# Another order for the opening steps of a fused attention and two-MLP kernel

## The chip, the cores and the metric

One core of a Trainium2 chip runs the whole program. The metric is device time in microseconds; lower is better. TensorE (PE) multiplies, VectorE (DVE), ScalarE (ACT) and GpSimd (POOL) do the rest, SyncE (SP) issues nearly all DMAs.

## The reference

```python
def _attn_ref(x, state):                      # x (4, 8, 512, 64), state (4, 8, 32, 64)
    a = softmax(scale * x @ state.T);   xread = a @ state
    a2 = softmax(scale * state @ x.T);  sread = a2 @ x
    return np.concatenate([xread, sread], axis=2)

x = attn_out.transpose(0, 2, 1, 3).reshape(2176, 512)
h = x @ w_in;   g = where(h >= 1, h, where(h <= -1, 0, (h + 1) ** 2 / 4));  x = g @ w_out   # 512 -> 2048 -> 512
h = x @ w_in2;  g = max(h, 0) + log1p(exp(-|h|));                           out = g @ w_out2
```

The four weights come as float64 and are read by the kernel as pairs of 32-bit words.

## The kernel before

**Windows.** The first MLP is done in tiles of 512 tokens (one for each of four batches and a small one), the second likewise. A tile is 16 windows of 128 hidden units. The attention of tile b is folded into the first product: for each pair p of W1 (256 hidden units) `g_mm` multiplies the state by W1 ("product p", L280), and `l1` of a window multiplies that product by the attention weights `ahi`, `alo` (L670). `l2` (L610 to L612) multiplies the activated window by W2 into four accumulators. Both products are taken in two parts, high and low: `copy` on ACT (L84) makes the high part, `sub` on DVE (L87) the low one. So product p gives `gh` and `gl`, an activated window `gth` and `gtl`, a W2 pair `wq` high and low.

**Weights.** A W1 or W2 pair (1 MB, numbered from 0) is loaded into a raw buffer, its high words are scaled by ACT (`scale`, L123), and `rebuild` on DVE shifts the low words (L138) and joins both (L139), each 128x1024. A W2 pair is then split into high and low (`split`). W1 pair p is needed by product p, W2 pair p by l2 of windows 2p and 2p+1.

**Order.** Nothing is left to a scheduler: each engine runs its instructions as they are emitted. Ahead of the loop stands block 0's attention (`f_sub` to `n_lo`) with `warm` matmuls on the identity between. Then the loop takes one step for each window i, and the lists in `ORDER` (L46) say in which order a step emits its parts: `l1` of window i, `open` (Relu and square on ACT, L759 and L760), `close` of window i-1 (the min/max on DVE, L775), `hi` and `lo` (gth, gtl of window i-1), `l2` of window i-2 (until step 14), the planned parts `early` (scale), `conv` (rebuild), `split`, `pe` (product, `place_state`) and `load`, and `hops`, pieces of the next block's attention (x transposes L305, their copies `xT`, block transposes L341 and L434, maxima and sums). `A1`, `A2` and `GW` hold the steps of the W1 pairs, the W2 pairs and the products; `HW` those of `place_state` and of the hops. The products, `place_state` (L267) and the x transposes all write the two PSUM banks of `side` (tile `at`), so each waits for the copies that empty it.

Of the kernel before, what the change touches and what calls it, by code (L numbers as in the profile page):

```python
# [10 lines left out]
F32R = mybir.dt.float32r  # L11
U32 = mybir.dt.uint32
AF = mybir.ActivationFunctionType
ALU = mybir.AluOpType
# [4 lines left out]
def fused_kernel(ctx: ExitStack, tc: tile.TileContext, x, state, w1, w2, w3, w4, out):  # L19
# [24 lines left out]
    LEAD = 14  # L44
    W_ = (7, 0, 4, 4, 4, 0, 8)
    ORDER = [  # L46
        "l1 post hops evac open close l2 early conv split hi late lo hops load pe".split(),
        "l1 post hops evac open close l2 hi split lo early conv late hops pe load".split(),
        "l1 post hops early evac open close l2 conv split hi late hops lo pe load".split(),
        "l1 post hops evac close l2 split early conv hi open late hops lo pe load".split(),  # L50
# [21 lines left out]
    def bank(tag, bufs):  # L72
        return new(psum, [P, 512], F32, tag, bufs)
# [24 lines left out]
    class Pair:  # L98
# [37 lines left out]
        def rebuild(self, v, raw):  # L136
            lo, hi, d = raw[:, 0::2], raw[:, 1::2], v.bitcast(U32)
            nc.vector.tensor_scalar(d, lo, 29, None, op0=ALU.logical_shift_right)  # L138
            nc.vector.scalar_tensor_tensor(d, hi, 3, d, op0=ALU.logical_shift_left, op1=ALU.bitwise_or)  # L139

# [23 lines left out]


    ident = new(p1, [P, P], F32, "ident")
    make_identity(nc, ident)
# [640 lines left out]

    GW = [1, 1, 2, 4, 6, 8, 10, 12]

# [3 lines left out]
    OWN = (3,)  # L814
    HW = [3, 0, 4, 15, 17]
    A1 = [-3, 0, 2, 3, 6, 6, 7, 12]
    A2 = [-1, 2, 4, 4, 8, 10, 13, 15]
    pairs, early = [], []
# [12 lines left out]
    for m, (a, pl) in enumerate(zip(at34, place)):  # L831
        w, inw, d = ((w3, True, W3), (w4, False, W4))[m % 2]
        plan_pair(Pair(w, inw, m // 2, d, lambda pl=pl: pools[pl]), a)
    pairs.sort(key=lambda t: t[0])


    room = [(-9, None), (-9, None)] + [(-9, p) for p in range(NP)]
    for n, (a, pair) in enumerate(pairs):
# [11 lines left out]
        if a == -3:  # L850
# [3 lines left out]
            continue  # L854
        when(*((a, "early") if a < NF else (a - 1, "late")), pair.scale)
        for k in range(n):
            when(a + k, "conv", lambda pair=pair, k=k, n=n: pair.conv(k, n))
        when(a + n, "split", pair.split)

# [45 lines left out]
    when(HW[0], "pe", lambda: place_state(st))  # L905
    when(0, "pe", lambda: warm(W_[5]))
    when(1, "pe", lambda: warm(W_[6]))
    for b, i0, i1 in ((1, HW[1], HW[2]), (2, NF + 3, NF + 6), (3, 2 * NF - 1, 2 * NF + 1)):
# [26 lines left out]
    with tc.manual_schedule():  # L935
# [31 lines left out]
        for g in range(NG):  # L967
            copy(hi[:, g, :], two[g][:, :C2])
        warm(W_[2], bank("acc0", 1))
        a0.scores()  # L970
        warm(W_[3], bank("acc0", 1))
        a0.f_norm(0, nc.gpsimd)
        a0.f_norm(1, nc.vector)
        run(-1, "early")
        for g in range(NG):
            a0.f_turn(g, bank(f"acc{g}", 1))
            a0.n_hi(g)
        for g in range(NG):
            sub(nc.vector, lo[:, g, :], two[g][:, :C2], f32(hi[:, g, :]))
        for g in range(NG):  # L980
            a0.s_copy(g)
        for g in range(NG):
            a0.n_lo(g, nc.vector)
        st = load_state()
        run(-1, "conv")
        run(-1, "load")

        for i in range(NW + LAG + 1):
# [6 lines left out]
            run(i, "start")  # L995
            for what in ORDER[min(i, 3) + (i >= NF)]:
                if what == "l1" and w is not None:
# [14 lines left out]
                elif what == "open" and w is not None:  # L1012
                    act_open(w)
                elif what == "hi" and v is not None:
                    cut_hi(v)
                elif what == "lo" and v is not None:
                    cut_lo(v)
                elif what in ("split", "early", "conv", "late", "pe", "load"):
                    run(i, what)
# [33 lines left out]
```

## Time and profile before

| what | us |
|---|---|
| median of 3 runs | 727.64 (727.11 to 727.82) |
| profiled execution | 727.26 |
| its span, first to last instruction | 725.5 |
| TensorE busy in the span | 715.2 (99%) |
| VectorE, ScalarE busy | 442.6 (61%), 443.6 (61%) |

Busy time of TensorE says little by itself: it counts warm-up matmuls and slow ones. What an edit of the opening can change is read from the timelines of the first 110 us: when TensorE stands, what ends the wait, and what DVE and ACT do in the meantime. In a row of a timeline, the bracket gives the idle time ahead of the group and what ended it.

### The profile page before, as it was taken

The page shows a single profiled execution, that of the slowest core. Times are in us where ns is not written, and L with a number is a line of the kernel's source. Part 1 is how long each engine was busy: PE and PEld are TensorE (multiplying, and loading weights), DVE is VectorE, ACT ScalarE, POOL GpSimd, SP SyncE. Part 2 cuts the span into 40 slices and gives each one's busy share as a digit, 9 for nine tenths or more (in the row PEclk, how much of TensorE's full clock was granted, in tenths as well). Part 3 has the DMA queues.
Part 4 walks back from the last instruction along what each step waited for, and adds up shares of the span by engine and source line. Part 5 has one row for each costly group of instructions (what it writes and reads, how often), then busy time and mean ns, then how long its engine had stood idle before and what let it go on. Part 6 is the DMA issues. An engine that isn't in the chain of part 4 may idle for free.

```text
span 725.5 us, 10280 instructions
## 1 busy us (share of the span) xinstructions
PE 715.2 (99%) x4054; PEld 579.2 (80%) x4054; DVE 442.6 (61%) x699; ACT 443.6 (61%) x730; POOL 17.9 (2%) x22
## 2 busy tenths in 40 slices
PE   8899999999999999999999999999999999999997
PEld 7577777778777887778888888888888888888886
DVE  5798875574684245777798756544555545544543
ACT  4787775555654356677887756555566556565553
POOL 0001200021000000000000000000000000000000
PEclk9999999999999999999999999999999999999999
DMA  9982005336160023353433011020002100010001
GB/s 335 349 276 104 1 0 116 61 68 108 59 175 1 1 63 112 131 174 116 148 144 130 23 37 58 11 63 0 1 1 78 39 0 1 1 58 1 1 0 59
DMA packets 61952, 56.31 MB, mean 78 GB/s; under 512 B 40976, under 2 KB 42832, under 8 KB 61904
## 3 DMA queue, kind: packets, MB, share of 16 engines
q1 hardware_dynamic: 61680, 55.46, 24.3%
q8 instruction: 32, 0.52, 0.3%
q10 hardware_dynamic: 224, 0.20, 0.1%
q14 instruction: 16, 0.13, 0.1%
HBM read 45.68 MB, written 9.96 MB: 77 GB/s over the span
## 4 chain that ended last, share of the span: by engine, by line
PE 91%; DMA 4%; DVE 2%; ACT 2%; issue 0%; SPq 0%; DVEq 0%; ACTq 0%
PE acc L610 16%; PE acc L612 16%; PE acc L611 16%; PE l L670 11%; PE l L610 9%; PE l L612 9%; PE l L611 9%; DMA wq<-in_moe_w_in_dram 3%; PE at L280 2%; PE l L657 2%; DMA ws<-in_moe_w_in_dram 1%; PE at L402 1%; ACT gh L84 0%; DVE cv L139 0%; DVE w L139 0%
## 5 line engine op out<-in xcount | busy, mean ns | idle before, releaser
L87 DVE TENSOR_TENSOR gtl<-tl,gth 128x512 fp32r<-128x512 f32 x64 | 44.3, 692 | 144.1 <-ACT gth L84 144.0
L768 ACT ACTIVATE ta<-l 128x512 f32<-128x512 f32 x68 | 40.7, 598 | 132.3 <-PE l L612 132.3
L610 PE MATMUL acc<-gth,wq 128*128 128x512 f32 x256 | 101.3, 396 | 0.0
L612 PE MATMUL acc<-gth,wq 128*128 128x512 f32 x256 | 99.8, 390 | 0.0
L611 PE MATMUL acc<-gtl,wq 128*128 128x512 f32 x256 | 99.7, 389 | 0.0
L87 DVE TENSOR_TENSOR gtl<-ta,gth 128x512 fp32r<-128x512 f32 x68 | 47.3, 695 | 66.4 <-ACT gth L84 66.4
L759 ACT ACTIVATE ta<-l 128x512 f32<-128x512 f32 x68 | 40.3, 592 | 46.7 <-PE l L670 30.2
L610 PE MATMUL acc<-wq,gth 128*128 128x512 f32 x152 | 59.2, 390 | 0.0
L611 PE MATMUL acc<-wq,gth 128*128 128x512 f32 x152 | 59.2, 389 | 0.0
L612 PE MATMUL acc<-wq,gtl 128*128 128x512 f32 x152 | 59.2, 389 | 0.0
L610 PEld LDWEIGHTS acc<-gth,wq 128*128 128x128 f32 x256 | 48.1, 188 | 12.5 <-issue 2.5
L612 PEld LDWEIGHTS acc<-gth,wq 128*128 128x128 f32 x256 | 48.0, 188 | 10.3
L611 PEld LDWEIGHTS acc<-gtl,wq 128*128 128x128 f32 x256 | 48.1, 188 | 9.5
L610 PE MATMUL acc<-wh,gth 128*128 128x512 f32 x136 | 52.9, 389 | 0.0
L611 PE MATMUL acc<-wl,gth 128*128 128x512 f32 x136 | 52.9, 389 | 0.0
L612 PE MATMUL acc<-wh,gtl 128*128 128x512 f32 x136 | 52.9, 389 | 0.0
L87 DVE TENSOR_TENSOR tl<-tl,ta 128x512 f32<-128x512 f32 x68 | 47.0, 691 | 2.4
L778 DVE SCALAR_TENSOR_TENSOR tl<-l,tl 128x512 f32<-128x512 f32 x68 | 46.4, 683 | 0.0
L779 DVE SCALAR_TENSOR_TENSOR ta<-tb,ta 128x512 f32<-128x512 f32 x68 | 46.3, 681 | 0.0
L775 DVE SCALAR_TENSOR_TENSOR ta<-ta,l 128x512 f32<-128x512 f32 x68 | 46.2, 679 | 0.0
L84 ACT ACTIVATE gth<-ta 128x512 fp32r<-128x512 f32 x68 | 42.1, 619 | 4.8 <-DVE ta L775 4.8
L771 ACT ACTIVATE tl<-tb 128x512 f32<-128x512 f32 x68 | 43.0, 633 | 2.2
(182 smaller groups left out, 1475.8 us busy)
## 6 DMA issues: line engine op xcount, KB each, us to landing
ws<-in_moe_w_in_dram SPq DMA_DIRECT2D x20, 512.0 KB, 4.6
ws<-in_moe_w_out_dram SPq DMA_DIRECT2D x20, 512.0 KB, 4.2
wq<-in_moe_w_in_dram SPq DMA_DIRECT2D x12, 512.0 KB, 8.9
wq<-in_moe_w_out_dram SPq DMA_DIRECT2D x12, 512.0 KB, 9.8
xd<-xs SPq DMA_DIRECT2D x16, 256.0 KB, 2.8
xs<-xd SPq DMA_DIRECT2D x16, 256.0 KB, 4.0
out_dram<-xs SPq DMA_DIRECT2D x15, 256.0 KB, 2.4
x<-in_x_dram SPq DMA_DIRECT2D x12, 256.0 KB, 4.5
```

The source lines that it names most:

```text
L84: nc.scalar.activation(dst, src, AF.Copy)
L87: eng.tensor_tensor(dst, a, b, op=ALU.subtract)
L610: nc.tensor.matmul(o, lh, rh, start=first, stop=False)
L611: nc.tensor.matmul(o, lh, rl, start=False, stop=False)
L612: nc.tensor.matmul(o, ll, rh, start=False, stop=last)
L670: nc.tensor.matmul(w.h, l[:, g, f], r[:, g, :], start=i == 0, stop=i == len(terms) - 1)
L759: nc.scalar.activation(w.a, w.hc, AF.Relu, bias=1.0)
L768: nc.scalar.activation(w.a, w.hc, AF.Abs)
L771: nc.scalar.activation(w.l, w.b, AF.Ln)
L775: nc.vector.scalar_tensor_tensor(w.a, w.a, 1.0, w.hc, op0=ALU.min, op1=ALU.max)
L778: nc.vector.scalar_tensor_tensor(w.l, w.hc, 0.0, w.l, op0=ALU.max, op1=ALU.add)
L779: nc.vector.scalar_tensor_tensor(w.a, w.b, 1.0, w.a, op0=ALU.subtract, op1=ALU.subtract)
```

## The change

The opening is emitted in another order, and the planned steps move. `ORDER` now has a list of its own for each of the steps 0 to 4; the lists for later steps are unchanged. In step 1 and 4 `l1` comes first, in steps 2 and 3 `l2`. `GW` puts products 1 and 2 one step later; `A1` and `A2` put W2 pair 3 from step 4 to 5, W1 pair 5 from 6 to 7 and W1 pair 6 from 7 to 9. `HW` puts `place_state` from step 3 to 5 and the hops of block 1 from 4 to 5. W1 pair 2 is loaded and rebuilt ahead of W2 pair 1. W1 pair 1's low words are shifted by ACT (`tail_act`, an ACTIVATE that reads the top byte of each low word, with a bias tile `off` that POOL sets), and the shift of W2 pair 0 stands ahead of the low parts of `alo`. The score copies `s_copy` move from ahead of the loop into step 1. The warm-up matmuls between product 0 and the scores, and those behind product 1, go; eight stand behind the scores and four at the end of step 1. Lines of the new kernel are shifted by 3 to 20 against those of the old.

```diff
@@ -10,6 +10,7 @@
 F32R = mybir.dt.float32r
 U32 = mybir.dt.uint32
+U8 = mybir.dt.uint8
 AF = mybir.ActivationFunctionType
 ALU = mybir.AluOpType
@@ -42,11 +43,13 @@
     LAG = 3
     LEAD = 14
-    W_ = (7, 0, 4, 4, 4, 0, 8)
+    W_ = (7, 8, 4)
     ORDER = [
-        "l1 post hops evac open close l2 early conv split hi late lo hops load pe".split(),
-        "l1 post hops evac open close l2 hi split lo early conv late hops pe load".split(),
-        "l1 post hops early evac open close l2 conv split hi late hops lo pe load".split(),
+        "l1 open load".split(),
+        "l1 close split hi open lo conv copy early load pe".split(),
+        "l2 close hi lo pe early l1 open conv split load".split(),
+        "l2 close hi lo pe split l1 open early conv load".split(),
+        "l1 close pe split early hi open lo l2 conv load".split(),
         "l1 post hops evac close l2 split early conv hi open late hops lo pe load".split(),
         "l1 post hops evac close l2 split early hops open hi late conv pe lo load".split(),
@@ -134,9 +137,18 @@
         def rebuild(self, v, raw):
-            lo, hi, d = raw[:, 0::2], raw[:, 1::2], v.bitcast(U32)
-            nc.vector.tensor_scalar(d, lo, 29, None, op0=ALU.logical_shift_right)
-            nc.vector.scalar_tensor_tensor(d, hi, 3, d, op0=ALU.logical_shift_left, op1=ALU.bitwise_or)
+            d = v.bitcast(U32)
+            self.tail(d, raw)
+            self.join(d, raw)
+
+        def tail(self, d, raw):
+            nc.vector.tensor_scalar(d, raw[:, 0::2], 29, None, op0=ALU.logical_shift_right)
+
+        def tail_act(self, d, raw):
+            nc.scalar.activation(d, raw.bitcast(U8)[:, 3::8], AF.Identity, scale=1.0 / 32, bias=off)
+
+        def join(self, d, raw):
+            nc.vector.scalar_tensor_tensor(d, raw[:, 1::2], 3, d, op0=ALU.logical_shift_left, op1=ALU.bitwise_or)
         def split(self):
@@ -163,6 +175,8 @@
+    off = new(p1, [P, 1], F32, "off")
+    nc.gpsimd.memset(off, 1.0 / 64 - 0.5)
     ident = new(p1, [P, P], F32, "ident")
     make_identity(nc, ident)
@@ -806,15 +820,15 @@
-    GW = [1, 1, 2, 4, 6, 8, 10, 12]
+    GW = [1, 2, 3, 4, 6, 8, 10, 12]
...
     TW.update({(3, p): 2 for p in range(0, NP, 2)})
     OWN = (3,)
-    HW = [3, 0, 4, 15, 17]
-    A1 = [-3, 0, 2, 3, 6, 6, 7, 12]
-    A2 = [-1, 2, 4, 4, 8, 10, 13, 15]
+    HW = [5, 0, 5, 15, 17]
+    A1 = [-3, 0, 2, 3, 6, 7, 9, 12]
+    A2 = [-1, 2, 4, 5, 8, 10, 13, 15]
     pairs, early = [], []
@@ -831,7 +845,8 @@
         w, inw, d = ((w3, True, W3), (w4, False, W4))[m % 2]
         plan_pair(Pair(w, inw, m // 2, d, lambda pl=pl: pools[pl]), a)
-    pairs.sort(key=lambda t: t[0])
+    pairs.sort(key=lambda t: (t[0], not t[1].inward))
+    second, third = (pairs[n][1] for n in (1, 2))
@@ -852,10 +867,13 @@
                 when(a, f"conv{i}", lambda pair=pair, i=i: pair.conv(i, 2))
             continue
-        when(*((a, "early") if a < NF else (a - 1, "late")), pair.scale)
-        for k in range(n):
-            when(a + k, "conv", lambda pair=pair, k=k, n=n: pair.conv(k, n))
-        when(a + n, "split", pair.split)
+        when(*((a - (a == 2 and pair.inward), "early") if a < NF else (a - 1, "late")), pair.scale)
+        if pair is third:
+            when(1, "conv", lambda: third.join(flat(third.v).bitcast(U32), third.raw))
+        elif pair is not second:
+            for k in range(n):
+                when(a + k, "conv", lambda pair=pair, k=k, n=n: pair.conv(k, n))
+        when(max(a + n, 1), "split", pair.split)
     def plan_g(i, b, p):
@@ -903,8 +921,8 @@
     aT0 = {}
     when(HW[0], "pe", lambda: place_state(st))
-    when(0, "pe", lambda: warm(W_[5]))
-    when(1, "pe", lambda: warm(W_[6]))
+    when(1, "pe", lambda: warm(W_[2]))
+    when(1, "copy", lambda: [a0.s_copy(g) for g in range(NG)])
     for b, i0, i1 in ((1, HW[1], HW[2]), (2, NF + 3, NF + 6), (3, 2 * NF - 1, 2 * NF + 1)):
         if b in BLOCKS:
@@ -966,23 +984,25 @@
         for g in range(NG):
             copy(hi[:, g, :], two[g][:, :C2])
-        warm(W_[2], bank("acc0", 1))
         a0.scores()
-        warm(W_[3], bank("acc0", 1))
+        warm(W_[1], bank("acc0", 1))
         a0.f_norm(0, nc.gpsimd)
         a0.f_norm(1, nc.vector)
         run(-1, "early")
+        run(0, "early")
+        third.v = W1[third.p] = new(p1, [P, NK, C2], F32, f"w1_{third.p}")
+        third.tail_act(flat(third.v).bitcast(U32), third.raw)
         for g in range(NG):
             a0.f_turn(g, bank(f"acc{g}", 1))
...
         for g in range(NG):
             sub(nc.vector, lo[:, g, :], two[g][:, :C2], f32(hi[:, g, :]))
-        for g in range(NG):
-            a0.s_copy(g)
+        second.v = new(base, [P, 1024], F32, "cv", 2)
+        second.tail(second.v.bitcast(U32), second.raw)
         for g in range(NG):
             a0.n_lo(g, nc.vector)
+        second.join(second.v.bitcast(U32), second.raw)
         st = load_state()
-        run(-1, "conv")
         run(-1, "load")
@@ -993,7 +1013,7 @@
             old = wins[i - LAG - 1] if i > LAG else None
             run(i, "start")
-            for what in ORDER[min(i, 3) + (i >= NF)]:
+            for what in ORDER[min(i, 5) + (i >= NF)]:
                 if what == "l1" and w is not None:
                     l1(w)
@@ -1015,7 +1035,7 @@
                 elif what == "lo" and v is not None:
                     cut_lo(v)
-                elif what in ("split", "early", "conv", "late", "pe", "load"):
+                elif what in ("split", "early", "conv", "late", "pe", "load", "copy"):
                     run(i, what)
             run(i, "end")
```

The first place is TensorE between the second and third window (`l`), with product 1 (`at<-w_1`), warm-up (`acc<-ident`) and l2 (`acc<-gth,wq`). Before:

```order
L670 MATMUL l_60_321<-ahi_129,gh_229 128x512 x2
L670 MATMUL l_60_321<-ahi_129,gl_230 128x512 x2
L670 MATMUL l_60_321<-alo_130,gh_229 128x512 x2
L280 MATMUL at_69<-w_1_56_309,stT_4_76 32x256 x8
L212 MATMUL acc_66_348<-ident_70 128x128 x8
L670 MATMUL l_67_357<-ahi_129,gh_344 128x512 x2
L670 MATMUL l_67_357<-ahi_129,gl_345 128x512 x2
L670 MATMUL l_67_357<-alo_130,gh_344 128x512 x2
L610 MATMUL acc_69_370<-gth_332,wq_57_312 128x512
```

And now, from the last matmuls of the first l2 on (its twelve, and four warm-ups ahead of them, follow the second window directly):

```order
L624 MATMUL acc_67_354<-gth_324,wq_57_321 128x512
L625 MATMUL acc_67_354<-gtl_325,wq_57_321 128x512
L626 MATMUL acc_67_354<-gth_324,wq_57_321 128x512
L294 MATMUL at_69<-w_1_48_272,stT_5_78 32x256 x8
L684 MATMUL l_72_376<-ahi_131,gh_371 128x512 x2
L684 MATMUL l_72_376<-ahi_131,gl_372 128x512 x2
L684 MATMUL l_72_376<-alo_132,gh_371 128x512 x2
L624 MATMUL acc_64_342<-gth_359,wq_57_321 128x512
```

The first l2 has moved ahead of product 1 and the third window, which it followed.

The second place is TensorE in steps 3 to 5: product 3 (`at<-w_3`) and `place_state` (`at<-ident,xs`). Before, in steps 3 to 4, `place_state` stood between l2 and window 4:

```order
L612 MATMUL acc_72_382<-gth_392,wq_57_312 128x512
L267 MATMUL at_69<-ident_70,xs_290 128x128 x4
L670 MATMUL l_87_453<-ahi_129,gh_404 128x512 x2
L670 MATMUL l_87_453<-ahi_129,gl_405 128x512 x2
L670 MATMUL l_87_453<-alo_130,gh_404 128x512 x2
L305 MATMUL at_69<-ident_70,x_58_315 128x128 x8
L610 MATMUL acc_69_370<-gth_438,wq_81_431 128x512
```

Now two windows follow product 2, and product 3 stands behind them, ahead of the l2 of window 2:

```order
L294 MATMUL at_69<-w_2_74_386,stT_5_78 32x256 x8
L684 MATMUL l_82_427<-ahi_131,gh_371 128x512 x2
L684 MATMUL l_82_427<-ahi_131,gl_372 128x512 x2
L684 MATMUL l_82_427<-alo_132,gh_371 128x512 x2
L684 MATMUL l_86_444<-ahi_131,gh_420 128x512 x2
L684 MATMUL l_86_444<-ahi_131,gl_421 128x512 x2
L684 MATMUL l_86_444<-alo_132,gh_420 128x512 x2
L294 MATMUL at_69<-w_3_84_438,stT_5_78 32x256 x8
L624 MATMUL acc_64_342<-gth_408,wq_81_424 128x512
```

Product 3 stood behind that l2 and the first x transposes. `place_state` now stands behind the first x transposes and l2 of window 3.

The third place is VectorE in steps 9 and 14. In step 9 (`gl` of product 5, min/max `ta`, low part of W2 pair 4 `wq`, then `gtl`) there stood:

```order
L87 TENSOR_TENSOR gl_708<-at_69,gh_707 128x512
L775 SCALAR_TENSOR_TENSOR ta_690<-ta_690,l_127_663 128x512
L87 TENSOR_TENSOR wq_137_731<-cv_684,wq_137_731 128x1024
L418 TENSOR_REDUCE mx_741<-sa_693 128x16
L87 TENSOR_TENSOR gtl_735<-ta_690,gth_734 128x512
```

And now:

```order
L90 TENSOR_TENSOR gl_695<-at_69,gh_694 128x512
L789 SCALAR_TENSOR_TENSOR ta_680<-ta_680,l_124_653 128x512
L90 TENSOR_TENSOR wq_133_718<-cv_674,wq_133_718 128x1024
L145 TENSOR_SCALAR w_6_134_722<-wq_85_441 128x1024
L151 SCALAR_TENSOR_TENSOR w_6_134_722<-wq_85_441,w_6_134_722 128x1024
L355 STREAM_TRANSPOSE sa_731<-xT_122_647 128x512
L432 TENSOR_REDUCE mx_733<-sa_683 128x16
L90 TENSOR_TENSOR gtl_726<-ta_680,gth_725 128x512
```

The rebuild of W1 pair 6 and a block transpose have come in ahead of `gtl`. In step 14 (low part of W2 pair 6, then `gtl` and the two `gl` of block 1's first products) there is now one row more:

```order
L90 TENSOR_TENSOR wq_169_911<-cv_889,wq_169_911 128x1024
L448 STREAM_TRANSPOSE sa_920<-sa_731 128x512
L90 TENSOR_TENSOR gtl_915<-ta_895,gth_914 128x512
L90 TENSOR_TENSOR gl_942<-at_69,gh_941 128x512
L789 SCALAR_TENSOR_TENSOR ta_917<-ta_917,l_168_903 128x512
L90 TENSOR_TENSOR gl_966<-at_69,gh_965 128x512
```

The transpose (`n_back` of the second group) stood in step 13, ahead of the `gtl` of that step.

## Rows read from the trace of the kernel before

**Rows 1.** TensorE's longest wait of the run: total us, times, longest us

```profile
PE at L280 <- DVE w L139: 2.8, 2, 2.3
```

**Rows 2.** TensorE's timeline: start us, us, engine, line, op, out<-in, count [idle before <-releaser]

```profile
25.37 0.67 PE L280 MATMUL at<-w,stT 64*32 64x256 f32 x16 [2.28 <-DVE w L139]
...
28.25 0.73 PE L670 MATMUL l<-ahi,gh 128*128 128x512 f32 x2 [0.23 <-ACT gh L84]
29.09 0.73 PE L670 MATMUL l<-ahi,gl 128*128 128x512 f32 x2
```

**Rows 3.** The same timeline from 30 to 45 us

```profile
30.12 0.40 PE L610 MATMUL acc<-gth,wq 128*128 128x512 f32 x1
...
30.82 0.39 PE L610 MATMUL acc<-gth,wq 128*128 128x512 f32 x1
...
38.38 0.60 PE L267 MATMUL at<-ident,xs 128*128 128x128 f32 x4
...
40.57 1.09 PE L305 MATMUL at<-ident,x 128*128 128x128 f32 x8 [0.21 <-DVE stT L268]
...
44.36 0.66 PE L280 MATMUL at<-w,stT 64*32 64x256 f32 x16
44.95 0.72 PE L670 MATMUL l<-ahi,gh 128*128 128x512 f32 x2
```

**Rows 4.** ScalarE's timeline, 15 to 28 us

```profile
15.57 1.15 ACT L123 ACTIVATE wq<-wq 128x1024 f32<-128x1024 f32 x1
19.16 1.09 ACT L84 ACTIVATE ahi<-acc 128x512 fp32r<-128x512 f32 x2 [2.44 <-PE acc L527]
...
21.77 0.60 ACT L759 ACTIVATE ta<-l 128x512 f32<-128x512 f32 x1 [0.54 <-PE l L670]
22.40 0.63 ACT L760 ACTIVATE ta<-ta 128x512 f32<-128x512 f32 x1
...
23.97 1.04 ACT L84 ACTIVATE wq<-cv 128x1024 fp32r<-128x1024 f32 x1
...
27.62 0.58 ACT L84 ACTIVATE gh<-at 128x512 fp32r<-128x512 f32 x1
```

**Rows 5.** VectorE's timeline, 25 to 32 us

```profile
25.24 1.22 DVE L87 TENSOR_TENSOR wq<-cv,wq 128x1024 fp32r<-128x1024 f32 x1
...
28.36 0.69 DVE L87 TENSOR_TENSOR gl<-at,gh 128x512 fp32r<-128x512 f32 x1
28.96 0.68 DVE L775 SCALAR_TENSOR_TENSOR ta<-ta,l 128x512 f32<-128x512 f32 x1
29.55 0.69 DVE L138 TENSOR_SCALAR cv<-wq 128x1024 uint32<-128x1024 uint32 x1
30.34 1.23 DVE L139 SCALAR_TENSOR_TENSOR cv<-wq,cv 128x1024 uint32<-128x1024 uint32 x1
31.49 0.69 DVE L138 TENSOR_SCALAR w<-wq 128x1024 uint32<-128x1024 uint32 x1
```

**Rows 6.** By stretch: us, busy us (instructions) of five engines, PEclk, DMA, GB/s

```profile
10.20:13.60 3.40, 2.85 (x47) 1.92 (x45) 3.19 (x9) 1.13 (x2) 0.00 (x0) 1.00 1.06 411
13.60:17.00 3.40, 3.40 (x40) 2.41 (x40) 3.23 (x9) 2.21 (x4) 1.05 (x1) 0.50 1.01 393
...
23.80:27.20 3.40, 1.83 (x27) 1.42 (x28) 2.96 (x3) 2.43 (x5) 0.00 (x0) 1.00 1.01 401
```

**Rows 7.** VectorE's timeline around step 9

```profile
63.91 0.70 DVE L341 STREAM_TRANSPOSE sa<-xT 128x512 f32<-128x512 f32 x1
...
67.24 1.22 DVE L87 TENSOR_TENSOR wq<-cv,wq 128x1024 fp32r<-128x1024 f32 x1
...
68.97 0.68 DVE L87 TENSOR_TENSOR gtl<-ta,gth 128x512 fp32r<-128x512 f32 x1
```

**Rows 8.** TensorE's timeline, the second matmul of l2(8) in step 10

```profile
71.04 0.39 PE L611 MATMUL acc<-gtl,wq 128*128 128x512 f32 x1
```

**Rows 9.** VectorE's timeline in step 14

```profile
90.90 0.68 DVE L87 TENSOR_TENSOR gtl<-ta,gth 128x512 fp32r<-128x512 f32 x1
91.66 0.69 DVE L87 TENSOR_TENSOR gl<-at,gh 128x512 fp32r<-128x512 f32 x1
```

**Rows 10.** TensorE's timeline, the start of window 17

```profile
98.52 0.73 PE L670 MATMUL l<-ahi,gh 128*128 128x512 f32 x2
```

## The prediction

> **What bounds the kernel now.** I read the waits of TensorE first. In the whole run it waits longest for the rebuilding of a W1 pair on VectorE (L139), and that wait lies in the opening [rows 1]. Where TensorE runs without pause an edit of the order gains nothing, so the change can act only through TensorE's pauses, and I read TensorE's timeline there. Behind the second window TensorE stands 2.28 us, does the product of W1 pair 1 at 25.37, fills the time with warm-up matmuls, and starts the third window at 28.25, whose second third waits for `gl` until 29.09 [rows 2]. Some 5 us hold 0.6 us of needed work. From 30 us on TensorE is nearly dense [rows 3]. What holds it there is the pair DVE and ACT, which convert weights while they serve the windows; so the change has to be followed on these two, in their order.
>
> **Start to second window.** The scores now come before the warm-up, so the transposes of `a0.f`, and with them the `ahi` copies, come a little earlier; I carry -0.2 us (bounds 0 and -0.3). ACT gets one operation more, the shift of W1 pair 1's low words, which no row shows. It lies between the shift on DVE, 0.69 [rows 5], and the scaling on ACT, 1.15 [rows 4]; I take 1.1, since it is an ACT operation of the same 128x1024. It and pair 1's scaling stand ahead of the `ahi` copies on ACT, where 2.44 us were idle [rows 4]: 16.7 + 1.1 + 1.1 = 18.9, just when the transposes end. Cover used up: at twice the price the first window would start 1 us later. The Trainium skill's page "ScalarE: Activation LUTs" (Rules for kernel authors) puts simple arithmetic on VectorE, and its section on ACT_TABLE_LOAD prices an ACTIVATE with a [128,1] bias so that I estimate 1.13 us here; by that rule the shift is a bad trade of 1.13 for 0.69. The trace says that ACT has the room at this one place, and the sum stays the same by either. The memset of `off` ahead of `ident` on POOL (0.1 us) is hidden, since x lands later. On SP W1 pair 2 goes ahead of W2 pair 1; no rebuild of rows 5 waits for a DMA, and W2 pair 1 is read later than before (about 32 in place of 29.55), so I cost it at nothing; if it were late, product 2 would not be, since W1 pair 2 is now the earlier one.
>
> **Second to third window.** In the new order TensorE does l2(0) first, then product 1, then window 2. Window 0 ended before when Relu began, at 21.77 [rows 4], so now at 21.5. Relu 0.6 and square 0.63 give 22.8; W2 pair 0's high copy 1.04 gives 23.7 [rows 4]; its low part on DVE 1.22 gives 25.0, and gtl(0), behind it, 25.6 [rows 5]. l2(0) can run from 25.65. Its matmuls come every 0.23 us [rows 3], so product 1 starts at 28.3. Its copy-out, 0.58 on ACT [rows 4] and 0.69 on DVE [rows 5], ends at 30.3, and window 2 ends at 31.4. Before, the same work (window 2 and l2(0)) ended at 30.12 + 2.75 = 32.9 [rows 3]. **Gain here 1.4 us.** The rebuild of pair 1 is no longer waited for; the wait goes to `gtl` (TensorE stands or warms from 22.8 to 25.6) and to product 1's copy-out (1 us).
>
> **Window 2 to product 3.** The new step 4 places product 3 ahead of l2(2), so TensorE meets W1 pair 3's rebuild early. TensorE gets there at 31.4 + l2(1) 2.8 + product 2 0.7 + windows 3 and 4 2.9 (six matmuls each) = 37.8. DVE stands at 29.6 with `gl` of product 1. After it come, in the spacing in which rows 5 show them (0.6 for a 512-wide operation, 0.79 from shift to join, 1.14 behind a 1024-wide one): gl 0.6; pairs W1 2 and W2 1, 2 x 1.93; min/max of window 2, 0.68; a round trip to ACT for gth(2), 0.7; gtl 0.6; gl of product 2, 0.6 and 0.3 of waiting for W2 1's high copy; its low part 1.14; shift and join of W1 3, 2.0, with 0.3 of waiting, because ACT scales pair 3 only behind the square of window 3. Sum 10.8, so 40.4. **A new pause of 2.6 us** (bounds 1.3 with none of the waiting, 3.0). At its end, 41.0, five windows, l2(0), l2(1) and products 1 to 3 are done. Before, this state with l2(2), `place_state` and the first x transposes on top (l2 2.9, place_state 0.4 and transposes 0.9 without their drains) was reached at 44.95, so 40.8 without them [rows 3]. **The 1.4 us are gone: level within 0.2** (bounds -1.3 and +0.4).
>
> **place_state.** It moves behind l2(3) of step 5. Its bank is shared with the x transposes that stand ahead of it now, and the order shows it waiting for ACT. That one wait covers a whole tile: before, the x transposes at 40.57 stood for the copy of `stT`, though it read the other bank [rows 3]. So it waits for both x copies. TensorE is there at 41.0 + 2.8 + 1.4 + 0.9 + 2.8 = 48.9. ACT: product 3's high copy 41.7, scaling of W2 2 42.75, gth(3) 43.35; DVE gtl(3) 44.0, W2 2 rebuilt 45.9; ACT again: its high copy, the scaling of W2 3, gth(4), Relu, square (1.04, 1.1, 0.6, 0.6, 0.63, less overlaps of 0.1) and two copies of 0.58 [rows 4]: 50.7. **+1.8 us** (bounds 0, +2).
>
> **Later pairs.** W1 pair 6 moves from step 7 to step 9 and block 1's hops come one step later. In step 9 DVE has `gl`, min/max and W2 4's low part, and now pair 6 (1.93) and a block transpose (0.70, next start 0.63) ahead of gtl(8). Before, gtl(8) ran from 68.97 [rows 7] to 69.65, and l2(8) read it at 71.04 [rows 8]: 1.35 us of slack against 2.56 added. **+1.2 us** (bounds 0.6, 1.3). In step 14 the second `n_back` and its `ahi` copy land between W2 6's low part and the copies of block 1's products: transpose 0.70 from 90.90, `ahi` 0.63, gh 0.58, so `gl` at 92.8 in place of 91.66 [rows 9]. DVE then runs without idle to the min/max that frees a window's bank, for which window 17 already stood at 98.52, 0.3 us late [rows 10]. **+1.1 us** (bounds 0, 1.2).
>
> **Sum.** 0 + 1.8 + 1.2 + 1.1 = 4.1 us on the profiled execution's 727.26 (a span of 725.5 and 1.8 around it, which the change doesn't touch): 731.4. That execution is 0.38 under the median of the three runs, so on the median it is 727.64 + 4.1 = **731.7 us**. The terms' bounds give -0.7 to +4.9.
>
> **Rivals.**
> Faster: VectorE and ScalarE catch up. The place is product 3: if W1 3's join is done when TensorE comes, at 37.8 instead of 40.4, 2.6 us stay won, place_state's chain starts as much earlier and the 1.8 us fall away; 4.1 - 2.6 - 1.8 = -0.3, and with the slack in steps 9 and 14 kept, -2.6: 725.0. For it: DVE loses one shift and idles some 2 us in handshakes. Against: the operations alone need 9.5 us from 29.6. Chance 0.12.
> No change: every handshake is there but shorter, the pause at product 3 is 1.5, place_state waits for one x copy only, and one of the two late terms is hidden: +0.4, 728.0. Chance 0.16.
> Slower still: the clock. TensorE's granted clock was 0.50, its lower level of 1.2 GHz, from 13.6 to 17.0, behind a stretch in which it was busy 2.85 of 3.40 us with small matmuls [rows 6]. Around the new pause at product 3 it would do little for 3.2 us. One such stretch at the lower level does half the work of 3.4 us: +1.7, so 733.4. Against: after standing 2.28 us the clock was still 1.00, though warm-up matmuls followed, which are absent here [rows 6]. Chance 0.17. The Trainium skill's page "TensorE: Matmul & The Clock Gate" (HAM oscillation) has idle gaps of TensorE bring back the half rate, and this rule speaks against a change that trades warm-up for a pause; the trace bears it out only in part, because the fall at 13.6 followed busy time.
>
> **How the numbers follow.** Forecast 0.55 (730 to 733.0), clock 0.17, no change 0.16, faster 0.12. The range of 8 in 10 leaves out the faster case, the lower part of the no-change case and the end of the clock case: 727.2 to 733.9. A measurement of this kernel tells about 0.2% (1.5 us) from nothing, so faster 0.12, same 0.16, slower 0.72.
>
> **What would show it.** Right: TensorE's waits name the rebuild of W1 pair 3 with over 2 us near 38 to 40, and ACT's x copy ahead of place_state with some 1.8; a wait for `gtl` in the eleventh step's l2 and a longer one ahead of window 17. Wrong: product 3 follows window 4 within 0.5 us, or window 2 ends later than 32 us, which would mean that the ACT shift delays `ahi`; or a second row of the lower clock.

## The result and the profile after

| what | before | after |
|---|---|---|
| median of five runs each, us | 727.11 | 733.33 (732.97 to 737.2) |
| ratio after / before | | 1.0095, 95% interval 1.0080 to 1.0111 |
| profiled execution, us | 727.26 | 732.97 |
| its span, us | 725.5 | 731.2 |

The change is slower by 0.95%, which is 5.8 to 8.1 us. The sum of the prediction was 4.1 us (0.56%). Executions differ in their opening by up to 4 us (last section), so medians and ratio are uncertain by some tenths of a per cent; the two profiled executions differ by 5.7 us, and these 5.7 us can be placed exactly, because TensorE runs the same matmuls in both, warm-up aside.

TensorE's longest waits after the change (engine, line, releaser: total us, times, longest us); the first one answers to [rows 1]:

```profile
PE at L294 <- DVE w L151: 2.4, 1, 2.4
PE acc L625 <- DVE gtl L90: 1.8, 2, 1.0
...
PE l L684 <- DVE ta L789: 1.1, 1, 1.1
PE l L684 <- ACT gh L87: 0.8, 1, 0.8
```

TensorE's timeline after (columns as in [rows 2]). The rows are, from the top: window 1; product 1; window 2; product 3; place_state; l2(5); window 8; the second matmul of l2(8); window 17; the last matmul:

```profile
21.18 0.63 PE L684 MATMUL l<-ahi,gh 128*128 128x512 f32 x2
...
28.22 0.66 PE L294 MATMUL at<-w,stT 64*32 64x256 f32 x16
29.64 0.74 PE L684 MATMUL l<-ahi,gh 128*128 128x512 f32 x2 [0.76 <-ACT gh L87]
...
40.31 0.67 PE L294 MATMUL at<-w,stT 64*32 64x256 f32 x16 [2.36 <-DVE w L151]
...
50.67 0.66 PE L281 MATMUL at<-ident,xs 128*128 128x128 f32 x4
...
59.50 0.50 PE L624 MATMUL acc<-gth,wq 128*128 128x512 f32 x1
...
62.36 0.39 PE L684 MATMUL l<-ahi,gh 128*128 128x512 f32 x1
...
74.16 0.50 PE L625 MATMUL acc<-gtl,wq 128*128 128x512 f32 x1 [0.97 <-DVE gtl L90]
...
102.93 0.72 PE L684 MATMUL l<-ahi,gh 128*128 128x512 f32 x2 [1.06 <-DVE ta L789]
...
726.85 0.39 PE L626 MATMUL acc<-wq,gtl 128*128 128x512 f32 x1
```

The same places in the kernel before: window 1, window 8 and the last matmul (window 17 is [rows 10]):

```profile
21.57 0.61 PE L670 MATMUL l<-ahi,gh 128*128 128x512 f32 x2
...
60.46 0.39 PE L670 MATMUL l<-ahi,gh 128*128 128x512 f32 x1
...
721.14 0.39 PE L612 MATMUL acc<-wq,gtl 128*128 128x512 f32 x1
```

So the lag of the changed kernel is 62.36 - 60.46 = 1.90 us at window 8, 102.93 - 98.52 = 4.41 at window 17, and 726.85 - 721.14 = 5.71 at the end. Three stretches, three amounts: 1.90, 2.51 and 1.30. In the last one TensorE has no new pause at all. There it takes 623.92 us for what took 622.62. At window 1 the changed kernel is 0.39 us ahead (21.18 against 21.57), so counted from there the first stretch is 2.29 and the whole 6.10.

All experiments were read in the same way. Since window 0 comes up to 4 us later in some executions than in others (last section), the table counts from window 1, not from the span's start. Each number is a difference of two starts on TensorE's timeline; "address" is how far the tiles behind `off` are moved.

| kernel | address, bytes | window 1 to 8 | window 8 to 17 | window 17 to last matmul |
|---|---|---|---|---|
| before | 0 | 38.89 | 38.06 | 622.62 |
| after | 32 | 41.18 | 40.57 | 623.92 |
| a1, `off` 64 bytes | 64 | 41.56 | 40.65 | 624.11 |
| b1, `off` 128 bytes | 128 | 41.60 | 40.59 | 623.60 |
| b2, `off` in x1s | 0 | 41.58 | 40.51 | 622.62 |
| a2, before + 4-byte tile | 32 | 39.06 | 38.19 | 623.92 |
| a3, W1 5 and 6 back | 32 | 42.10 | 39.32 | 623.94 |
| b3, product 3 late | 32 | 43.88 | 40.59 | 623.94 |
| b4, warm-up in the pause | 32 | 41.18 | 40.57 | 623.95 |
| c1, hops from step 4 | 32 | 41.79 | 43.28 | 623.94 |
| c2, place_state in step 3 | 32 | 42.75 | 40.59 | 623.88 |
| c3, shift on VectorE | 32 | 41.34 | 40.59 | 623.92 |
| h1, place_state in step 1 | 32 | 53.71 | 40.59 | 623.94 |
| h3, hops ahead from step 11 | 32 | 41.58 | 42.36 | 623.93 |
| g1 = b2 + a3 + c1 | 0 | 42.11 | 41.96 | 622.64 |
| k1 = b2 + a3 + h1 + b3 | 0 | 56.87 | 39.18 | 622.64 |
| k2 = b2 + a3 + h1 + b4 | 0 | 55.30 | 39.18 | 622.62 |
| r1 = b2 + a3 | 0 | 41.66 | 39.18 | 622.62 |
| r2 = r1 + pair 3 earlier | 0 | 40.57 | 39.18 | 622.61 |

### The profile page after: what moved, and what is told of

It is laid out like the page before. It is cut to its first block, busy times and chain, and to the rows that moved or that the text cites. A ratio compares the mean times of both kernels' runs of the same rounds, so it can differ in the third digit from the quotient of the medians.

```text
span 731.2 us, 10263 instructions
## 1 busy us (share of the span) xinstructions
PE 716.4 (98%) x4046; PEld 578.8 (79%) x4046; DVE 442.7 (61%) x698; ACT 444.7 (61%) x731; POOL 17.9 (2%) x23
## 4 chain that ended last, share of the span: by engine, by line
PE 91%; ACT 4%; DVE 3%; issue 1%; DMA 1%; POOL 0%; DVEq 0%; ACTq 0%; POOLq 0%
PE acc L624 16%; PE acc L625 16%; PE acc L626 16%; PE l L684 11%; PE l L626 8%; PE l L625 8%; PE l L624 8%; PE at L294 2%; PE l L671 2%; DVE cv L151 1%; ACT gh L87 1%; ACT wq L126 1%; DMA wq<-in_moe_w_out_dram 1%; PE at L416 1%; PE acc L226 0%
```

## The experiments

**The last 1.30 us: addresses.** `off` is a tile of 4 bytes per partition, allocated ahead of `ident` in the pool that also holds W1, `gh`, `gl` and half of `ahi` and `alo`. It takes 32 bytes there, and all tiles behind it move by that. Four kernels vary this alone.

```diff
-    off = new(p1, [P, 1], F32, "off")
+    off = new(p1, [P, 16], F32, "off")[:, :1]     # a1; b1 has [P, 32]
```

> The changed kernel with the bias tile `off` 64 bytes wide per partition in place of 4, so that every tile behind it in the same pool (ident, stT, W1, gh, gl, half of ahi and alo) starts on a multiple of 64 bytes again, as before; nothing else differs. In the changed kernel TensorE falls behind the kernel before by a further 1.8 us between 60 and 335 us beside the pauses, in small pieces (matmuls every 0.229 us in place of 0.227), and no more behind 335, where that pool is closed. Theory: the 32 bytes by which `off` moved these tiles cost this; then the pieces are gone, the lag at the end falls from 5.7 to some 3.9 us and the median by 1.8 us. Rival: the pieces come from other work lying beside the matmuls; then the lag stays at 5.5 or more.

> The changed kernel with `off` 128 bytes wide per partition, so that the tiles behind it in its pool are moved by 128 bytes in place of 32 (64 in a1, which kept the slow matmuls). Theory: the matmuls' extra time depends on where the tiles start against a grid, and 128 is on it: from 60 to 335 us TensorE's lag grows by 0.3 us or less beside the pauses, in place of 1.8, and the end comes 1.5 us earlier. Rival: the grid is coarser than 128 bytes, or it is the distance to the other tiles that counts: the lag grows by 1.5 or more as in a1.

```diff
-    off = new(p1, [P, 1], F32, "off")
     ...
     x1s = new(p1, [P, NJ, B * N], F32, "x1s")
+    off = x1s[:, 0, :1]                            # b2
```

> The changed kernel with no tile of its own for the bias: it stands in the first column of x1s, which is written only much later. All tiles of that pool have the addresses of the kernel before. Theory of the addresses: from 60 to 335 us the lag grows by 0.3 us or less beside the pauses (1.8 in the changed kernel), some 1.5 us less at the end. Rival (the changed order of work beside the matmuls): 1.5 or more as in the changed kernel.

```diff
+    off = new(p1, [P, 1], F32, "off")              # a2, on the kernel before
+    nc.gpsimd.memset(off, 1.0 / 64 - 0.5)
     ident = new(p1, [P, P], F32, "ident")
```

> The kernel before with one 4-byte tile (set by GpSimd, read by nobody) ahead of ident, which moves the same tiles by 32 bytes; order and work unchanged. Theory of the 32 bytes: 1.5 to 2 us slower than before, growing evenly from 30 to some 330 us, no new pause of TensorE over 0.2 us. Rival (other work beside the matmuls in the changed order): within 0.3 us of before.

Window 17 and the last matmul on TensorE's timeline, in a2 (the kernel before, shifted) and then in b2 (the changed kernel, not shifted):

```profile
98.34 0.72 PE L672 MATMUL l<-ahi,gh 128*128 128x512 f32 x2
...
722.26 0.39 PE L614 MATMUL acc<-wq,gtl 128*128 128x512 f32 x1
```

```profile
103.50 0.73 PE L684 MATMUL l<-ahi,gh 128*128 128x512 f32 x2 [1.06 <-DVE ta L789]
...
726.12 0.39 PE L626 MATMUL acc<-wq,gtl 128*128 128x512 f32 x1
```

722.26 - 98.34 = 623.92 and 726.12 - 103.50 = 622.62: with the order of before and the addresses of after the stretch takes what it takes after, and with the order of after and the addresses of before what it takes before. All eleven kernels of the table and the text that move the tiles by 32 bytes take 623.88 to 623.95, all seven that leave them in place 622.61 to 622.64. So the addresses are the cause. A shift of 64 bytes costs 1.5, one of 128 bytes 1.0, so my guess of a 64-byte grid was wrong, and that of a 128-byte one too. How the address slows a matmul, and whether a coarser grid or the distance to other tiles counts, is open. The medians are too coarse for it: a2 took 1.0017 of before, with an interval (0.9998 to 1.0036) that includes 1.

**W1 pair 6 and l2(8).**

```diff
-    A1 = [-3, 0, 2, 3, 6, 7, 9, 12]
+    A1 = [-3, 0, 2, 3, 6, 6, 7, 12]
```

> The changed kernel with W1 pairs 5 and 6 in steps 6 and 7 again (A1 as before), all else as changed. Theory: the 0.98 us pause of TensorE at l2(8) (74.2) goes, and with it some 1.0 us of the lag; window 17's pause of 1.06 stays, since its chain starts in step 14. Rival: DVE is late anyway, and the pause moves to another window or l2 within 10 us, lag unchanged within 0.3.

The pause at l2(8) went, and window 8 to 17 fell by 1.25 us. But the rebuild of pair 5, now a step earlier, sits ahead of the block-1 scores, which wait 0.38 us for `gl`, and window 8 comes 0.92 later; 0.4 of that is another course of the clock, as in a1, b1 and b2 (41.6 for 41.2, below); in r1, which has this edit and no fall of the clock there, it is 0.48. To the last matmul 0.3 us are left of 1.25, or 0.7 without the clock's part. The cause of the pause is shown; undoing it alone is worth little.

**What window 17 waits for.** A first kernel, a4, set `HW[2]` to 4 alone. The list of step 4 has no word `hops`, so its program was the changed kernel's, and it serves as a second look at the changed kernel: 0.97 at l2(8), 1.05 at window 17, both again. c1 adds the word. In it `place_state` falls between the second x transposes and their copies and overwrites one bank, so block 1's attention is computed from other data there (in g1 too); kind and number of the instructions are the same.

```diff
-        "l1 close pe split early hi open lo l2 conv load".split(),
+        "l1 close pe split early hi open lo l2 hops conv load".split(),   # c1
-    HW = [5, 0, 5, 15, 17]
+    HW = [5, 0, 4, 15, 17]
```

> The changed kernel with block 1's hops from step 4 on: HW[2] is 4 and the list of step 4 has the word hops behind l2 (a4 lacked it there, so its program was that of the changed kernel). Every hop, the block transposes and ahi copies too, comes one step earlier, as in the kernel before. Counted from window 1's first matmul, window 17 starts at 81.75 us in the changed kernel. Theory (the second n_back in step 14 is what window 17 waits for): its pause of 1.05 falls to 0.3 or less, and that at l2(8) of 0.98 to some 0.4, together some 1.3 us; the opening stays within 0.4. Rival: DVE is late at window 17 for the whole way since step 5; the pause stays at 0.8 or more.

```diff
+            if i == 11:                               # h3
+                for g in gens:
+                    next(g, None)
             run(i, "end")
```

> The changed kernel with one hop more at the end of step 11, so that block 1's later hops come one step earlier: the second n_back is in step 13, as before, and everything up to step 11 is unchanged. Window 17 waits 1.06 us in the changed kernel. Theory (n_back in step 14 is what it waits for): 0.3 or less, and the end 0.7 to 0.9 us earlier. Rival (VectorE's whole load from step 9 on): 0.7 or more, or the pause moves to another window between 13 and 18.

TensorE's pauses between window 13 and window 17 in h3:

```profile
86.72 0.67 PE L294 MATMUL at<-w,stT 64*32 64x256 f32 x16 [0.70 <-DVE w L151]
94.71 0.73 PE L684 MATMUL l<-ahi,gh 128*128 128x512 f32 x2 [0.56 <-DVE ta L789]
97.25 0.50 PE L626 MATMUL acc<-gth,wq 128*128 128x512 f32 x1 [0.42 <-DVE wq L90]
104.73 0.50 PE L684 MATMUL l<-ahi,gh 128*128 128x512 f32 x1 [0.80 <-DVE ta L789]
```

The second `n_back` is in step 13 here, and window 17 still waits 0.80, with three new pauses before it; window 8 to 17 takes 1.8 us more than in the changed kernel. c1 shows the same three kinds of pause (1.17, 0.56 and 0.42), waits 0.81 at window 17, and its pause at l2(8) grew to 1.46 where some 0.4 was expected. So the theory that this one transpose is to blame falls as a remedy. I read it so that VectorE has too little slack from step 11 to 16, and what is taken out of step 14 is missing in another step; no run takes work away from VectorE there. The chain itself is there in the changed kernel's VectorE, as the prediction drew it: transpose, then `gl` behind `ahi` and `gh`, then no idle time over 0.13 us up to the min/max for which window 17 waits.

```profile
94.19 0.70 DVE L448 STREAM_TRANSPOSE sa<-sa 128x512 f32<-128x512 f32 x1
94.82 0.64 DVE L90 TENSOR_TENSOR gtl<-ta,gth 128x512 fp32r<-128x512 f32 x1
96.07 0.69 DVE L90 TENSOR_TENSOR gl<-at,gh 128x512 fp32r<-128x512 f32 x1 [0.61 <-ACT gh L87]
...
102.19 0.68 DVE L789 SCALAR_TENSOR_TENSOR ta<-ta,l 128x512 f32<-128x512 f32 x1
```

**The first 1.90 us: product 3, the clock, place_state.** In the changed kernel the granted clock fell to 0.50 (1.2 GHz) behind the pause at product 3, which was a rival of the prediction (us, busy us of PE, PEld, DVE, ACT, POOL, PEclk, DMA share, GB/s):

```profile
41.40:44.70 3.30, 3.30 (x10) 2.52 (x9) 2.09 (x4) 2.95 (x5) 0.00 (x0) 0.50 0.98 379
44.80:48.20 3.40, 3.40 (x20) 2.87 (x20) 2.87 (x4) 2.34 (x3) 0.00 (x0) 1.00 0.53 192
```

b4 fills the pause (a warm-up matmul is two rows of the trace, so nine are x18), b3 takes it away.

```diff
+    when(4, "pe", lambda: warm(9, side[:, 0, :]))    # b4, ahead of the products
```

> The changed kernel with nine warm-up matmuls on the identity ahead of product 3, in its pause. Theory: they fit in the pause (2.1 of 2.36 us), TensorE's clock stays full behind product 3, l2(2) takes 2.8 us in place of 4.6, and TensorE stands ahead of place_state for 1.5 to 1.9 us instead: l2(5) at 59.5 plus or minus 0.3, nothing won. Rival (the slow clock is what costs): l2(5) at 58.2 or earlier, 1.3 us won.

```diff
-        "l1 close pe split early hi open lo l2 conv load".split(),
+        "l1 close split early hi open lo l2 pe conv load".split(),        # b3
```

> The changed kernel with product 3 behind the l2 of window 2 in step 4, as the kernel before had it; place_state stays in step 5. Theory (VectorE and ScalarE set the end, TensorE's pause only shows it): the pause of 2.36 us ahead of product 3 falls under 0.3, the clock doesn't fall behind it, but the x copies come no earlier than at 50.7, so place_state waits 3 us or more and l2(5) starts at 59.5 plus or minus 0.5 (from a window start at 18.97 us), nothing won. Rival (the order on TensorE is the cause): l2(5) comes at 58 or earlier, 1.5 us or more won to the end.

TensorE in b4 (warm-up, product 3, place_state) and the clock behind product 3 there:

```profile
37.33 2.17 PE L226 MATMUL at<-ident 128*128 128x128 f32 x18
39.89 0.67 PE L294 MATMUL at<-w,stT 64*32 64x256 f32 x16 [0.39 <-DVE w L151]
...
50.22 0.66 PE L281 MATMUL at<-ident,xs 128*128 128x128 f32 x4 [1.67 <-ACT xT L87]
```

```profile
40.60:48.50 7.90, 7.90 (x38) 6.27 (x38) 5.69 (x8) 6.33 (x9) 0.00 (x0) 1.00 0.79 290
```

The clock stays full, l2(2) is done sooner, and TensorE stands 1.67 us ahead of `place_state`, in place of 0.13 (the l2 ended at 50.54). Window 8 is at 41.18 in both. The slow clock cost nothing here, since it lay in time in which TensorE would have waited for the x copies. In a1, b1 and b2 it began 1.2 us earlier (18.9 to 19.0 us behind window 1 in place of 20.15), and window 8 came at 41.6; so it did in h3 (18.7), whose edit acts only from step 11 on. I take it that there only a part lay in that time. In b3 it is otherwise: the pause goes to `place_state`, and behind it the clock is at 0.50 for twice as long, now over work for which everything is ready:

```profile
49.89 1.12 PE L281 MATMUL at<-ident,xs 128*128 128x128 f32 x4 [2.76 <-ACT xT L87]
```

```profile
49.10:55.90 6.80, 6.01 (x20) 5.17 (x21) 5.56 (x8) 5.16 (x9) 0.00 (x0) 0.50 0.51 166
```

`place_state` itself starts 29.4 us behind window 1 in b3 and 29.5 in the changed kernel, so the x copies come no earlier, and all of the loss lies behind it. Window 8 comes 2.7 us later. Nothing won, as expected, but I had not expected the loss.

Two kernels put `place_state` elsewhere.

```diff
-    HW = [5, 0, 5, 15, 17]
+    HW = [3, 0, 5, 15, 17]            # c2
+    HW = [1, 0, 5, 15, 17]            # h1, which also moves load_state() behind the first loads
```

> The changed kernel with place_state in step 3 again, behind product 2. Counted from window 1's first matmul, window 8 starts at 41.18 us in the changed kernel and at 38.89 before. Theory of the prediction (TensorE loses 1.8 us because place_state waits behind the x copies): window 8 at 39.4 to 39.9. Rival (the handshakes of VectorE and ScalarE from product 3 on set the time, and place_state only shows it): its wait goes to the next l2 or window, and window 8 stays at 40.7 or later.

> The changed kernel with place_state in step 1, ahead of the warm-up matmuls there, where TensorE waits for gtl(0) anyway; for that the state is loaded right behind the first pairs. Counted from window 1's first matmul, product 1 starts at 7.05 us, product 3 at 19.13 and window 8 at 41.18 in the changed kernel. Theory of the prediction (place_state behind the x copies costs 1.8): window 8 at 39.4 or earlier. Rival (ScalarE's chain behind product 3 sets the time, place_state only shows it): its 0.4 us of matmuls and 0.1 of waiting go, window 8 at 40.5 to 40.9, and product 3 stays at 19.1. A third case: the state's DMA delays the weights, and product 1 comes later than 7.5.

c2 doesn't decide it: behind product 2, `place_state` waits 2.01 us for that product's copy-out, the pause at product 3 stays at 2.20, and window 8 is 1.6 us late. h1 met its third case in another form:

```profile
PE at L281 <- DMA xs<-in_state_dram: 13.6, 1, 13.6
PE at L294 <- DVE w L151: 2.4, 1, 2.4
...
PE at L294 <- ACT xT L87: 0.8, 1, 0.8
```

The state's four DMAs are issued from 25.0 us on, behind ten pairs, as in the changed kernel (25.6), so TensorE stood 13.6 us. What comes behind can still be read: product 1 to window 8 takes 33.11 us, against 62.36 - 28.22 = 34.14 in the changed kernel and 34.14 in b4, where the clock is full in that stretch as here. That is 1.0 of the 1.8 us, and TensorE now waits 0.8 at the next product for an x copy. In k2 (below), which has the same place of `place_state`, product 1 to window 8 takes 34.17, only 0.4 less than the 34.57 of r1, and that next wait is 1.8. So 0.4 to 1.0 us hang on `place_state`, and most of the wait moves on.

**The ACT shift.**

```diff
-        third.tail_act(flat(third.v).bitcast(U32), third.raw)
+        third.tail(flat(third.v).bitcast(U32), third.raw)
```

> The changed kernel with W1 pair 1's low words shifted by VectorE at the place where ScalarE did it. Theory: the ACT shift (1.26 us) is hidden and so is the DVE shift (0.69) in its place, since VectorE has idle time ahead of n_lo; window 0 within 0.2 us, product 1 at 7.0 plus or minus 0.3 us behind window 1, the end within 0.3 us of the changed kernel. Rival A: ScalarE's shift delays ahi, and window 0 comes 0.3 to 0.7 us earlier without it. Rival B: VectorE is the bound already here, and product 1 comes 0.5 to 0.7 us later.

Product 1 comes 7.05 us behind window 1 in both, so rival B falls. The profiled executions of c3 and a4 have the same slow opening, and window 0 starts at 23.83 and 23.68: there the shift is hidden on either engine. But ScalarE had 0.44 us to spare ahead of the `ahi` copies in a4, and none in the changed kernel's profiled execution, where TensorE's opening was faster. There they start 0.81 us behind the first transpose (18.80 - 17.99), against 0.67 before and 0.66 in a4. So the shift can cost some 0.15 us in a fast opening; no run of c3 was profiled in one.

**Together.** g1 (b2, a3 and c1) took 1.0073 of before, and k1 and k2 (b2, a3 and h1, with product 3 late or warm-up ahead of it) 1.0219 and 1.0220, since each held an edit with a cost of its own: c1's pauses, h1's 13.6 us. All three missed what was expected: g1's last matmul 3.2 us earlier than in the changed kernel, counted from window 1 (it came 1.0 later), window 8 by 40.5 in k1 and 39.6 in k2 (56.87 and 55.30). Their third stretch is 622.62 to 622.64 and so bears out b2 three times more. r1 holds b2 and a3 alone. r2 shortens the chain of VectorE and ScalarE where it begins:

```diff
+        if a == 3 and pair.inward:                    # W1 pair 3
+            def shift(pair=pair):
+                pair.v = W1[pair.p] = new(p1, [P, NK, C2], F32, f"w1_{pair.p}")
+                pair.tail_act(flat(pair.v).bitcast(U32), pair.raw)
+            when(2, "load", pair.scale)
+            when(3, "split", shift)
+            when(3, "conv", lambda pair=pair: pair.join(flat(pair.v).bitcast(U32), pair.raw))
+            continue
```

> The changed kernel with the bias in x1s (b2) and W1 pairs 5 and 6 in steps 6 and 7 (a3), nothing else. Theory: the two add up. TensorE's end, counted from window 1's first matmul, at 703.2 us plus or minus 0.4 (705.67 in the changed kernel, 699.57 before), the median 2.6 us under the changed kernel's, 0.5% above the kernel before. Rival: they overlap, 704.2 or later.

> r1 with W1 pair 3's scaling moved to the end of step 2, where ScalarE has 1.9 us free, and its shift done by ScalarE in step 3 behind W2 pair 1's high copy, so that VectorE has only the join ahead of product 3. Theory (the chain of VectorE and ScalarE from W1 pair 3's rebuild on sets the time): the join starts 0.6 to 1.0 us earlier, product 3 at 18.1 to 18.6 behind window 1 (19.1 in r1), window 8 earlier by 0.5 to 1.0, and that much at the end. Rival (ScalarE is the bound): its two more operations delay gth, gh and the Relu, product 3 comes at 18.8 or later, or window 8 is not earlier.

Product 3, place_state and window 8 on TensorE, in r1 and then in r2 (window 1 starts at 20.44 and 20.60):

```profile
39.61 0.67 PE L294 MATMUL at<-w,stT 64*32 64x256 f32 x16 [2.36 <-DVE w L151]
49.92 0.66 PE L281 MATMUL at<-ident,xs 128*128 128x128 f32 x4 [1.73 <-ACT xT L87]
...
62.10 0.39 PE L684 MATMUL l<-ahi,gh 128*128 128x512 f32 x1
```

```profile
38.67 0.67 PE L294 MATMUL at<-w,stT 64*32 64x256 f32 x16 [1.31 <-DVE w L151]
48.99 0.66 PE L281 MATMUL at<-ident,xs 128*128 128x128 f32 x4 [1.73 <-ACT xT L87]
...
61.17 0.39 PE L684 MATMUL l<-ahi,gh 128*128 128x512 f32 x1
```

r1: last matmul at 703.46 behind window 1 (expected 703.2), median 731.23, 1.0052 of before (1.0034 to 1.0071). The two add up. r2: product 3 comes 1.10 us earlier (18.07 for 19.17), place_state 1.09, window 8 1.09, the last matmul 1.10 (702.36). The whole chain moves with the rebuild of W1 pair 3, and the wait for the x copies stays at 1.73, so VectorE and ScalarE set the time here, as the theory said. Median 729.87, 1.0029 of before (1.0010 to 1.0048). Behind window 1, 2.79 of the 6.10 us are left, and no kernel of this study beats the one before. At window 8 r2 is still 1.68 late (40.57 against 38.89); 0.48 of that comes with a3's edit, and the rest is not taken apart.

## Why the prediction was right in its direction and too small in its sum

**Start to second window: right in place, small in price.** The ACT shift took 1.26 us, over its forecast of 1.1 and over its upper bound of 1.15. It used up the cover, as forecast, and held the `ahi` copies by some 0.15 us; they began at 18.80 in place of 19.16 [rows 4], and window 0 started 0.38 us earlier (forecast 0.2). Some of that can be luck: before, the granted clock was 0.50 from 13.6 to 17.0 [rows 6], and in this execution it was 1.00.

```profile
17.64 1.26 ACT L148 ACTIVATE w<-wq,off 128x1024 uint32<-128x1024 uint8 x1
18.80 1.05 ACT L87 ACTIVATE ahi<-acc 128x512 fp32r<-128x512 f32 x2
...
49.55 1.07 ACT L87 ACTIVATE xT<-at 128x512 f32<-128x512 f32 x2
```

**Second window to product 3: right.** Product 1 came at 28.22 (28.3), window 2 ended at 31.4 (31.4), product 3 started at 40.31 (40.4), behind a pause of 2.36 (2.6) for the join of W1 pair 3.

**place_state: right in size, half right in cause.** The x copies ended at 50.6 (50.7). TensorE came later than forecast, because its clock fell, and waited only 0.13 us; l2(5) started 1.78 us late all the same (1.8). So one sign of being right, a wait of some 1.8 for the x copy, was absent, and one of being wrong, a second row of the lower clock, came. The clock rival added 1.7 to the sum, and b4 shows that the two don't add here: a slow TensorE eats a wait that it would have had. That its 733.4 lies beside the measured median is luck. And the cause is the chain of VectorE and ScalarE behind W1 pair 3 (r2), of which the place of place_state is 0.4 to 1.0 (k2, h1).

**Later pairs: right.** 0.97 us at l2(8) (1.2), 1.06 - 0.15 = 0.91 at window 17 (1.1); with what is lost in starting again, window 8 to 17 took 2.51 us more, against 1.2 + 1.1. For l2(8) a3 shows the cause. For window 17 the trace shows the chain, but taking out the step that I blamed doesn't help (h3), so the cause there is in part open.

**The step that failed is the one about `off`:** "The memset of `off` ahead of `ident` on POOL (0.1 us) is hidden". I priced the instruction that the diff adds, and not the 32 bytes by which its tile moves every tile behind it in its pool. That cost 1.30 us from window 17 on (a2 puts another 0.3 ahead of it, mixed with the clock), and no term or rival had it. Without it, the sum of 4.1 stands against 1.90 + 2.51 = 4.41. On the median shown before, 1.0095 is 734.6 us, and the range ended at 733.9. The 5.71 us of the profiled execution alone would give 733.35, inside it; most of the other 1.2 us come from two of the five executions, 735.19 and 737.2, whose traces are not kept. Without the 1.30, or without these two, the time would lie in the range. So the miss comes from the failed step and in part from chance.

One sum of the prediction doesn't come out: the conditions of the no-change rival, priced by its own terms (1.1 for the pause, 0.6 for one x copy, 1.1 or 1.2 for a late term), leave some 1.2 us and not 0.4. The result doesn't hang on it.

## What to carry to other kernels

A new tile can move what is allocated behind it: compare the tiles' addresses as well as the order; here it helped to put the constant into a tile that is written later (b2). Where two engines hand work to each other in turn, a pause of the third may only show their chain: here moving the pause (b3, c2) or filling it (b4) won nothing, and what shortened the chain at its head (r2) was still won at the end. And moving one operation out of a full step may only move the wait (h3).

## What the runs showed of the hardware

**Tile addresses cost TensorE time.** From window 17 on no new wait appears, every engine runs as many instructions, and the same 622.62 us of work take 623.60 to 624.11 when the tiles of one pool are moved by 32, 64 or 128 bytes. For a single matmul it is 1.5 ns in the mean: between 115 and 330 us the mean step from one matmul of 512 columns to the next (steps of 0.215 to 0.240 us) is 0.2274 us before and 0.2289 after, and from 500 us on, where that pool is closed, 0.2267 in both.

**The clock behind a pause.** Behind a pause of 2.36 us at product 3 the granted clock fell to 0.50 (1.2 GHz) for 3.4 us in the changed kernel, and stayed at 1.00 (2.4 GHz) in r1 behind the same pause of 2.36, which ended at 39.61 (columns as in [rows 6]):

```profile
37.00:40.00 3.00, 0.64 (x18) 0.19 (x16) 2.65 (x4) 1.29 (x2) 0.00 (x0) 1.00 1.10 245
40.00:44.00 4.00, 4.00 (x33) 3.15 (x18) 2.25 (x5) 3.26 (x5) 0.00 (x0) 1.00 0.99 352
```

Before, [rows 6] had shown a stretch without a fall after 2.28 us; a2, with the same order, fell to 0.50 from 26.2 to 29.6 at that place. So one pause can go either way. The Trainium skill's page "TensorE: Matmul & The Clock Gate" (HAM oscillation) says that idle gaps bring back the half rate. Behind the pauses of the changed kernel (2.36 us), of a2 (2.24) and of b3 (2.76) it came back, behind those of r1 and of the kernel before it didn't.

**A slow opening.** In the profiled executions of a1, a4 and c3 TensorE's small matmuls took nearly twice as long up to some 20 us, and window 0 started at 23.6 to 23.8; in the changed kernel's it started at 19.4. The two groups of score matmuls, in the changed kernel and then in a4, whose program is the same:

```profile
8.10 1.98 PE L256 MATMUL at<-stT,xT 64*128 64x32 f32 x32
9.90 1.95 PE L256 MATMUL l<-stT,xT 64*128 64x32 f32 x32
```

```profile
9.43 3.63 PE L256 MATMUL at<-stT,xT 64*128 64x32 f32 x32
12.87 3.60 PE L256 MATMUL l<-stT,xT 64*128 64x32 f32 x32
```

It looks like the lower clock, but the rows don't show it: the granted clock stands at 1.00 in a4, too, from 12 to 21 us. So the cause is open. a4's profiled execution took 737.21 us, as much more than the changed kernel's 732.97 as its window 0 came later (4.2). The highest times of other kernels lie about as far above their lowest, of the kernel before too (731.65 against 726.77 in one set of runs), so the change alone doesn't bring it; whether it makes it more frequent is not shown.
